# First batch of a softmax-off-by-one attention with a maxout feed-forward: denominators inverted by VectorE out of PSUM instead of by ScalarE's logarithm and exponential

## The chip, the cores and the metric

One core of one Trainium2 chip. The metric is the device time of one execution in microseconds (us); of several executions the median is given. Engines are named as in the profile: PE is TensorE, DVE is VectorE, ACT is ScalarE, POOL is GpSimd, SP is the sync engine. L12 means line 12 of the kernel before.

## What is computed

Attention over 8 batches of 12 heads, 448 positions, 64 wide, with one added to the softmax's denominator, and then a feed-forward that takes the largest of three projections. Inputs and output are f32.

```python
scores = scale * np.matmul(q, k.transpose(0, 1, 3, 2))
m = np.max(scores, axis=-1, keepdims=True)
e = np.exp(scores - m)
attn = e / (np.sum(e, axis=-1, keepdims=True) + np.exp(-m) + 1e-09)
x = np.matmul(attn, v)                      # -> (8 * 448, 768)
h = np.maximum(np.maximum(x @ w1, x @ w2), x @ w3)
out = h @ w_out
```

Multiplied through by exp(m), the denominator is the sum of exp(score) plus one, so the kernel needs no maximum. It computes exp(score) / 8 (`EDIV` = 8), so the one that is added is 1/8, and it scales the inverse by `LAMBDA` = 256, which the last step takes out again.

## The kernel before

The heads are taken in groups of four: 24 groups, three to a batch, numbered 0 to 23. Of each group the four heads lie two and two on the 128 partitions, so that four matmuls on 64 x 64 quarters of PE make one tile of scores.

The program is written out in order, without a scheduler: each engine does its instructions in the order in which the Python code issues them. Three stretches follow each other. The first (up to about 37 us) is batch 0, groups 0 to 2, written out as a list of two-letter steps (`start`, L664). The second and third do groups 3 to 23 with projection pieces in between, and a last stretch does the end of the feed-forward.

The change touches only the first stretch. There each group is done in two parts, query columns 0 to 191 and 192 to 447 (`PARTS`), so that the feed-forward of the first columns can start early. A part's steps, with the group and the part as the digits behind them:

- `S` (`scores_part`, L407): up to two score tiles into a pair of PSUM banks (`stp`), then one exponential on ACT (L419) into `eTp`. Seven tiles make four such units.
- `G` (`pair_sum`, L428): DVE adds pairs of exponentials into `eP` (L437), so that PE has fewer terms to add. One such sum in a part 0, two in a part 1.
- `D` (`den_part`, L444): PE adds up the terms by matmuls with a matrix of ones (L345), five terms of four matmuls in a part 0 and three in a part 1, into a pair of banks (`dps`, called `den`). Then ACT takes the logarithm of the sum plus 1/8 (L463) and the exponential of minus that, times 256 (L466), into `rb`, in SBUF.
- `N` (`num_part`, L471): PE multiplies exponentials with values (`num`), and DVE multiplies the result by `rb` into `xT` (L493). In a part 0 `num` lies in two single banks, in a part 1 in a pair.
- `M` (`moe`, L614): the next piece of the projections (`up_part`, L528; matmuls L537 into the single bank `p_i`, taken out by DVE at L546 or L548). A piece needs `xT` of all three groups of batch 0 for its part. The first `M1` stands after `N20`, the last numerator of part 0.
- `T` (`pe_transpose_both`, L232): transposes of keys and queries by PE, copied out by DVE (L252, L257).
- `U` and `E`: scores and sums of group 3 and later, in another form (L297, L321, L331).

The order of the steps around the change:

```python
I S000 S001 S002 S003 T1 G001 S100 S101 T2 S102 D00 G101 S103 N00 S200 S201 D10 S202 N10 G201
S203 S010 D20 S011 N20 S012 G011 S013 M1 G012 S110 S111 M1 D01 S112 G111 S113 M1 G112 N01 S210
S211 M1 D11 G211 T3 S212 S213 G212 N11 U301 M1 D21 U32 N21 M1 E312 U334 M1 T41 E334 U356 M1 E356
```

PSUM has eight banks. Two are single banks (`ps1`), shared by `trT`, `num` of part 0, `p_i` and the warm-up. Six are three pairs (`double`, L85) that are given out in turn: each score unit, denominator and part-1 numerator takes the next pair, and must wait until the reader of what lay there three turns before is done. So a denominator's pair comes free when the instruction that reads `den` ends.

Before all that, 92 matmuls on constants (L161) run while the first loads are under way. Loads are issued from POOL's queue and, for the first keys, from SP's and ACT's.

From group 3 on the denominators are inverted by `den_group` and `recip_group` (L365, L372), also a logarithm and an exponential on ACT. The change leaves those as they are.

Of the kernel before, what the change touches and what calls it, by code (L numbers as in the profile page):

```python
# [12 lines left out]
AF = mybir.ActivationFunctionType  # L13
# [3 lines left out]
MMDT = FP16  # L17
LAMBDA = 256.0
EDIV = 8.0
# [3 lines left out]
def kernel(  # L23
# [11 lines left out]
    nc = tc.nc  # L35

    B, H, S, D = q.shape
    NTOK, DM = out.shape
    DFF = moe_w1.shape[1]
    KC = 64  # L40
# [5 lines left out]
    scale = 1.0 / math.sqrt(D)  # L46
# [5 lines left out]
            name=nc.get_next_instruction_name(),  # L52
# [6 lines left out]
    cpool = ctx.enter_context(tc.tile_pool(name="const", bufs=1))  # L59
# [21 lines left out]
    def single(name, shape=(512,), dtype=FP32):  # L81
        return ps1.tile([128, *shape], dtype, tag="bank1", name=name)


    def double(name, shape=(512,), dtype=FP32):  # L85
        turn[0] += 1
        n = turn[0] % len(pair_pools)
        return pair_pools[n].tile([128, 2, *shape], dtype, tag=f"pair{n}", name=name)
# [62 lines left out]
    load_group(2, "v")  # L151
    ones16 = cpool.tile([128, KC], MMDT, name="ones16")
    nc.vector.memset(ones16, 1.0)
    WQ, WN = 23, 208
    warm16 = cpool.tile([128, S], MMDT, name="warm16")
    nc.vector.memset(warm16, 1.0)
    warm = [single("warm") for _ in range(2)]
    for _ in range(WQ):
        for r in range(2):
            for c in range(2):  # L160
                nc.tensor.matmul(  # L161
                    out=warm[r][c * KC : c * KC + KC, 0:WN],
                    lhsT=ones16[r * KC : r * KC + KC],
                    rhs=warm16[r * KC : r * KC + KC, 0:WN],
                    start=True,
                    stop=True,
                )
# [50 lines left out]
    def half(n):  # L218
        return slice(n * KC, n * KC + KC)
# [123 lines left out]
    def av_tiles(outs, weights, moving, start, stop):  # L343
        for r, c in TILES:
            nc.tensor.matmul(  # L345
                out=outs[r][half(c)],
                lhsT=weights(r, c),
                rhs=moving(r, c),
                start=start,
                stop=stop,  # L350
            )
# [92 lines left out]
    def den_part(i, part):  # L444
        st = state[i]
        q0, q1 = PARTS[part]
        nq = (q1 - q0) * KC
        eT = st["eT", part]
        dps = double("den")
        terms = [eT[:, j] for j in range(NJ)]  # L450
        if "eP" in st:
            eP, n = st.pop("eP")
            terms = [eP[:, 0], eP[:, 1]] + terms[n:]
        for n, e in enumerate(terms):
            av_tiles(
                [dps[:, r, 0:nq] for r in range(2)],
                lambda r, c: ones16[half(r)],
                lambda r, c: e[half(r), c],
                n == 0,
                n == len(terms) - 1,  # L460
            )
        rb = small.tile([128, 2, S], FP32, tag="rb", name="rb")
        nc.scalar.activation(  # L463
            out=rb[:, :, 0:nq], in_=dps[:, :, 0:nq], func=AF.Ln, bias=1.0 / EDIV
        )
        nc.scalar.activation(  # L466
            out=rb[:, :, 0:nq], in_=rb[:, :, 0:nq], func=AF.Exp, bias=math.log(LAMBDA), scale=-1.0
        )
        st["rb", part] = rb

    def num_part(i, part):  # L471
# [176 lines left out]
    def sums(i, *units):  # L648
# [6 lines left out]
        "T": pe_transpose_both,  # L655
        "S": scores_part,
        "D": den_part,
        "N": num_part,
        "M": moe,
# [298 lines left out]
    for i in range(MID, NI + 1):  # L958
        for op, j, w in ORDER if i > MID else ORDER[4:]:
            if op == "U" and i < NI:  # L960
                for_pair()
                mm = visit([(i, j)])
                n, name = ((2, "v"), (3, "k"), (3, "q"), (0, ""))[j // 2]
# [19 lines left out]
            if op == "N":  # L983
                for_pair()
                pair = num_group(i - 1)
                n = turn[0] % 2
# [206 lines left out]
    def last_piece(c0, c1, cuts, end=None):  # L1193
        def done(bank):
            nc.vector.tensor_scalar(
                out=o_last[:, c0:c1],
                in0=bank[:, 0 : c1 - c0],
                scalar1=1.0 / LAMBDA,
                scalar2=None,
                op0=ALU.mult,  # L1200
            )
            if end is not None:
                store(LATE, NT - 1, o_last[:, end], end, (nc.sync, nc.scalar))

        return plain(B // 2 - 1, NT - 1, c0, c1, cuts, done)
# [24 lines left out]
    for n in range(4):  # L1230
# [3 lines left out]
    e = (  # L1234
        last_piece(0, NW, (3,), slice(0, NW))
        + last_piece(NW, NW + NW // 2, ())
        + last_piece(NW + NW // 2, DM, (), slice(NW, DM))
    )
# [37 lines left out]
```

## Time and profile before

| what | us |
|---|---|
| median of 3 runs | 319.5 |
| lowest and highest of them | 318.58, 319.5 |
| the profiled execution, its own time | 318.78 |
| its span, from the first to the last instruction | 317.0 |
| first and last L463 start | 14.0, 34.3 |
| first and last L466 start | 14.5, 34.9 |
| last L493 start | 35.9 |
| granted TensorE clock | 1.000 |

Rows of the profile read: line, engine, operation, output <- inputs, number of instructions, busy time, mean duration of one in ns, the idle time of that engine just before, and what ended it. In rows in order of time the first two figures are the start and the length of a merged stretch. Six executions of L463 (502 to 629 ns) and six of L466 (522 to 630 ns) are what is replaced.

### The profile page before, as it was taken

The page shows a single profiled execution, that of the slowest core. Times are in us where ns is not written, and L with a number is a line of the kernel's source. Part 1 is how long each engine was busy: PE and PEld are TensorE (multiplying, and loading weights), DVE is VectorE, ACT ScalarE, POOL GpSimd, SP SyncE. Part 2 cuts the span into 40 slices and gives each one's busy share as a digit, 9 for nine tenths or more (in the row PEclk, how much of TensorE's full clock was granted, in tenths as well). Part 3 has the DMA queues.
Part 4 walks back from the last instruction along what each step waited for, and adds up shares of the span by engine and source line. Part 5 has one row for each costly group of instructions (what it writes and reads, how often), then busy time and mean ns, then how long its engine had stood idle before and what let it go on. Part 6 is the DMA issues. An engine that isn't in the chain of part 4 may idle for free.

```text
span 317.0 us, 12721 instructions
## 1 busy us (share of the span) xinstructions
PE 303.0 (96%) x5605; PEld 232.5 (73%) x5605; DVE 235.1 (74%) x434; ACT 229.6 (72%) x308; POOL 100.5 (32%) x173
## 2 busy tenths in 40 slices
PE   7679999999999999999999999999999999999993
PEld 6567777658779877788878897898887775555562
DVE  3546598999888768877776778788866746987953
ACT  1899859987778786788778986878889664654350
POOL 8967666640232332233222332333000000000040
PEclk9999999999999999999999999999999999999999
DMA  7999999999489998889995999689800052000176
GB/s 144 168 189 197 204 207 187 157 179 162 60 119 114 176 173 119 121 120 225 121 128 68 189 177 197 74 131 189 171 4 2 2 134 70 1 0 2 50 201 199
DMA packets 59927, 40.64 MB, mean 128 GB/s; under 512 B 32832, under 2 KB 56864, under 8 KB 59872
## 3 DMA queue, kind: packets, MB, share of 16 engines
q0 software_dynamic: 25680, 21.80, 48.9%
q1 hardware_dynamic: 33648, 17.21, 26.7%
q8 instruction: 44, 0.72, 1.0%
q10 hardware_dynamic: 544, 0.82, 0.8%
q14 instruction: 11, 0.09, 0.1%
HBM read 42.47 MB, written 11.01 MB: 169 GB/s over the span
## 4 chain that ended last, share of the span: by engine, by line
PE 84%; ACT 7%; issue 2%; DMA 2%; DVE 2%; POOL 1%; DVEq 0%; POOLq 0%
PE piece L785 42%; PE stp L297 9%; PE bank_a L1028 8%; PE av L345 8%; PE bank_s L1028 6%; PE p_i L537 4%; ACT eTp L419 3%; PE piece L537 2%; ACT eT L321 2%; PE bank_a L1173 2%; DMA ld_q<-in_q_dram 2%; PE den L345 1%; PE piece L560 1%; ACT rb L463 1%; DVE eS L331 1%
## 5 line engine op out<-in xcount | busy, mean ns | idle before, releaser
L321 ACT ACTIVATE eT<-stp 128x896 f16<-128x896 f32 x147 | 132.3, 918 | 33.6 <-PE stp L297 31.7
L785 PE MATMUL piece<-xT,w 64*64 64x448 f16 x2160 | 134.9, 349 | 0.4 <-DVE xT L400 0.3
L785 PEld LDWEIGHTS <-w 64*64 64x64 f16 x2160 | 93.3, 107 | 17.7 <-issue 2.8
L331 DVE TENSOR_TENSOR eS<-eS,eT 128x896 f16<-128x896 f16 x105 | 65.2, 621 | 12.5 <-ACT eT L321 10.7
L297 PE MATMUL stp<-qkT 64*64 64x448 f16 (+2 forms) x756 | 69.3, 332 | 2.3 <-ACT eTp L419 0.8
L785 PE MATMUL piece<-w,hT 64*64 64x384 f16 x792 | 48.7, 323 | 0.4 <-DVE hT L526 0.4
L526 DVE TENSOR_TENSOR hT<-hT,piece 128x448 f16<-128x448 f16 x60 | 37.1, 619 | 14.9 <-PE piece L785 12.0
L112 POOL DMA_DIRECT2D ld_q<-in_q_dram x48 | 28.9, 609 | 53.8 <-PE stp L297 24.1
L112 POOL DMA_DIRECT2D ld_v<-in_v_dram x48 | 28.5, 597 | 43.1 <-PE stp L297 25.1
L297 PEld LDWEIGHTS <-qkT 64*64 64x64 f16 x756 | 30.8, 106 | 11.3 <-issue 5.7
L785 PEld LDWEIGHTS <-hT 64*64 64x64 f16 x792 | 34.9, 107 | 4.5 <-issue 1.1
L112 POOL DMA_DIRECT2D ld_k<-in_k_dram x46 | 27.7, 608 | 23.6 <-PE stp L297 10.3
L345 PE MATMUL av<-eT,ld_v 64*64 64x448 f16 x588 | 33.0, 349 | 0.5 <-issue 0.5
L345 PEld LDWEIGHTS <-ld_v 64*64 64x64 f16 x756 | 27.3, 107 | 6.1 <-issue 1.4
L586 POOL DMA_DIRECT2D out_dram<-o x7 | 3.7, 536 | 84.0 <-DMA out_dram<-o_sb 79.3
L400 DVE TENSOR_TENSOR xT<-av,rb 128x448 f16<-128x448 f32 x42 | 24.2, 618 | 7.0 <-PE piece L785 3.5
L365 ACT ACTIVATE rb<-den 128x896 f32<-128x896 f32 x21 | 19.3, 918 | 5.6 <-PE den L345 5.5
L419 ACT ACTIVATE eTp<-stp 128x768 f16<-128x768 f32 (+3 forms) x24 | 18.0, 821 | 7.4 <-PE stp L297 7.3
L537 PEld LDWEIGHTS <-w 128*128 128x128 f16 x216 | 18.9, 98 | 5.2 <-issue 3.5
L372 ACT ACTIVATE rb<-rb 128x896 f32<-128x896 f32 x21 | 20.1, 955 | 0.2
L1028 PEld LDWEIGHTS <-comb 128*128 128x128 f16 x108 | 10.6, 98 | 9.9
L331 DVE TENSOR_TENSOR eS<-eT 128x896 f16<-128x896 f16 x21 | 13.0, 621 | 5.9 <-ACT eT L321 5.8
(102 smaller groups left out, 333.9 us busy)
## 6 DMA issues: line engine op xcount, KB each, us to landing
out_dram<-o_sb SPq DMA_DIRECT2D x42, 192.0 KB, 4.1
ld_q<-in_q_dram POOLq DMA_DIRECT2D x48, 112.0 KB, 4.3
ld_v<-in_v_dram POOLq DMA_DIRECT2D x48, 112.0 KB, 4.1
ld_k<-in_k_dram POOLq DMA_DIRECT2D x46, 112.0 KB, 4.2
w<-in_moe_w_dram POOLq DMA_DIRECT2D x6, 192.0 KB, 7.0
w<-in_moe_w_out_dram POOLq DMA_DIRECT2D x3, 384.0 KB, 7.5
w<-in_moe_w_dram POOLq DMA_DIRECT2D x2, 384.0 KB, 6.7
out_dram<-o SPq DMA_DIRECT2D x8, 96.0 KB, 3.0
```

What stands on the lines that cost most here:

```text
L112: return eng.dma_start(out=dst[hp * KC : hp * KC + KC].rearrange("p s j d -> p s (j d)"), in_=src[:, half_heads(name, hp)],)
L297: mm = nc.tensor.matmul(out=out[half(c), r], lhsT=qkT[half(r), 0, j, h], rhs=qkT[half(r), 1, q0:q1, h], start=True, stop=True,)
L321: nc.scalar.activation(out=st["eT"][:, j], in_=stp[:, :, 0:S], func=AF.Exp, scale=scale, bias=-math.log(EDIV))
L331: nc.vector.tensor_tensor(out=st["eS"], in0=st["eT"][:, 0] if j == 1 else st["eS"], in1=st["eT"][:, j], op=ALU.add,)
L345: nc.tensor.matmul(out=outs[r][half(c)], lhsT=weights(r, c), rhs=moving(r, c), start=start, stop=stop,)
L372: nc.scalar.activation(out=st["rb"], in_=st["rb"], func=AF.Exp, bias=math.log(LAMBDA), scale=-1.0)
L400: nc.vector.tensor_tensor(out=xT[b][:, 2 * g + r, :], in0=banks[r][:, 0:S], in1=state[i]["rb"][:, r], op=ALU.mult)
L419: nc.scalar.activation(out=eT[:, j0 : j0 + n].rearrange("p j r q -> p r j q"), in_=stp[:, :, 0 : n * nq].rearrange("p r (j q) -> p r j q", ...
L526: nc.vector.tensor_tensor(out=dst, in0=dst, in1=p_i[:, 0:S], op=ALU.max)
L537: nc.tensor.matmul(out=p_i[:, ts(j, nq)], lhsT=w_sb[i][:, dc, ts(2 * fp + j, 128)], rhs=xT[b][:, dc, q0 * KC : q1 * KC], start=(dc == 0), ...
L785: nc.tensor.matmul(out=p["bank"][half(c), 0:w], lhsT=lhs(k, r, c), rhs=rhs(k, r), start=(r == p["first"] and k == 0), stop=(r != p["first" ...
L1028: nc.tensor.matmul(out=bank, lhsT=lhs(k), rhs=rhs(k), start=start and k == 0, stop=k == 2, skip_group_check=True,)
```

## The change

The six pairs of ACT instructions in `den_part` go, and one DVE reciprocal, which reads the denominators in PSUM and writes `rb` in SBUF as f32, stands in their place. The 1/8 that the logarithm's bias added is now added by PE: a further term, ahead of the others, multiplies two constant tiles, and since 1/256 is folded into the matrix that was ones, the reciprocal gives the scaled inverse directly. Two new constant tiles are set by DVE at the start; the wider one also serves the warm-up matmuls, in place of the tile of 448 ones.

```diff
     ones16 = cpool.tile([128, KC], MMDT, name="ones16")
     nc.vector.memset(ones16, 1.0)
+    inv16 = cpool.tile([128, KC], MMDT, name="inv16")
+    nc.vector.memset(inv16, 1.0 / LAMBDA)
     WQ, WN = 23, 208
-    warm16 = cpool.tile([128, S], MMDT, name="warm16")
-    nc.vector.memset(warm16, 1.0)
+
+    one16 = cpool.tile([128, 4 * KC], MMDT, name="one16")
+    nc.vector.memset(one16, 1.0 / EDIV / KC)
...
-                    rhs=warm16[r * KC : r * KC + KC, 0:WN],
+                    rhs=one16[r * KC : r * KC + KC, 0:WN],
...
-        for n, e in enumerate(terms):
+        for n, e in enumerate([None, *terms]):
             av_tiles(
                 [dps[:, r, 0:nq] for r in range(2)],
-                lambda r, c: ones16[half(r)],
-                lambda r, c: e[half(r), c],
+                lambda r, c: inv16[half(r)],
+                lambda r, c: one16[half(r), 0:nq] if e is None else e[half(r), c],
                 n == 0,
-                n == len(terms) - 1,
+                n == len(terms),
             )
         rb = small.tile([128, 2, S], FP32, tag="rb", name="rb")
-        nc.scalar.activation(
-            out=rb[:, :, 0:nq], in_=dps[:, :, 0:nq], func=AF.Ln, bias=1.0 / EDIV
-        )
-        nc.scalar.activation(
-            out=rb[:, :, 0:nq], in_=rb[:, :, 0:nq], func=AF.Exp, bias=math.log(LAMBDA), scale=-1.0
-        )
+        nc.vector.reciprocal(out=rb[:, :, 0:nq], in_=dps[:, :, 0:nq])
```

No step changes its place in the list. In DVE's order the first reciprocal now stands ahead of G101's sum, the second ahead of group 1's `xT`, and each of the others between the pair sums, `hT` and `xT` instructions where `den_part` issues it.

## Prediction

> **What bounds the kernel now.** I read the page's head first, then the windows of the first 72 us, then the chain of waits of 10 to 40 us, then VectorE's and ScalarE's rows in order of time, since the change touches only the first batch. The head:
>
> ```profile
> span 317.0 us, 12721 instructions
> PE 303.0 (96%) x5605; PEld 232.5 (73%) x5605; DVE 235.1 (74%) x434; ACT 229.6 (72%) x308; POOL 100.5 (32%) x173
> ```
>
> Over the whole span TensorE (PE) is the bound. By stages (columns: stretch, its length, busy time of PE, weight loads, VectorE, ScalarE, GpSimd, granted clock, DMA share, GB/s):
>
> ```profile
> 13.70:21.20 7.50, 5.04 (x185) 3.92 (x179) 2.67 (x9) 7.41 (x14) 5.30 (x9) 1.00 1.21 175
> 21.20:36.70 15.50, 14.96 (x297) 11.59 (x296) 10.47 (x21) 14.67 (x21) 11.52 (x19) 1.00 1.25 198
> 36.70:72.00 35.30, 34.18 (x610) 23.95 (x609) 31.46 (x58) 28.93 (x35) 20.56 (x34) 1.00 1.15 186
> 72.00:260.00 188.00, 187.04 (x3990) 156.36 (x3986) 144.05 (x265) 148.05 (x188) 47.42 (x80) 1.00 0.79 123
> ```
>
> The reader is to see that the change falls in the first two rows. ScalarE is full there (22.1 of 23.0 us), VectorE has 13.1 of 23.0 busy, so 9.9 us free. From 36.7 us on PE is busy all but about 2 us of 223: what delays PE's work before 36.7 us comes out at the end nearly whole, and what is gained there is kept. The chain of waits within 10 to 40 us agrees:
>
> ```profile
> by line: ACT eTp L419 37.0%; PE p_i L537 18.6%; DMA ld_q<-in_q_dram 17.2%; issue 11.7%; ACT rb L463 7.6%; PE stp L297 7.5%; ACT rb L466 5.8%; PE den L345 3.1%; PE num L345 2.5%; DVE qkT L257 2.1%; PE trT L223 2.0%; PE trT L228 1.9%
> ```
>
> L463 and L466 are the logarithm and exponential that the change removes: 13.4% of that stretch's chain.
>
> **Removed from ScalarE.** Six pairs. One pair takes 0.97 us (384 columns, 14.01 to 14.98) or 1.2 us (512 columns, 24.72 to 25.91); read off the starts of what follows, the six sum to 6.5 us.
>
> **Added on PE.** One more term of four matmuls per part, ahead of the others. In the timeline 28 matmuls of 192 columns take 0.77 us and 28 of 256 take 0.93 to 0.96 us, so four cost 0.11 and 0.14 us: 3 x (0.11 + 0.14) = 0.75 us in all. They read constants alone and need only a free bank pair, so in the first three parts they lie in PE's waits (2.46 us idle before 21.2); the other three, 0.4 us, lie on PE. The new constants' two memsets (64 and 256 columns) stand for one of 448 columns (0.43 us at 0.98 us); the first data come at 5.25 us, so they cost nothing.
>
> **Added on VectorE: six reciprocals out of PSUM, three of 384 and three of 512 columns.** No row of this trace divides on VectorE, so the cost is bounded. One pass over the same columns is the conversion out of PSUM:
>
> ```profile
> L546 DVE CAST hT<-p_i 128x512 f16<-128x512 f32 x3 | 2.1, 692 | 1.5 <-PE p_i L537 1.4
> ...
> L546 DVE CAST hT<-p_i 128x384 f16<-128x384 f32 x3 | 1.7, 558 | 1.4 <-PE p_i L537 1.4
> ```
>
> The difference gives (692 - 558) / 128 = 1.05 ns per column and pass; the next instruction starts 0.47 us after the short one (22.35 to 22.82 us), so 0.07 us is fixed. Lower end: one pass, 0.47 and 0.61 us, six for 3.2 us. Upper end: a quotient to full f32 put together from multiplies and subtracts. From a start value good to about 4 bits, three Newton steps (4, 8, 16, more than 24 bits) of three operations are nine passes. In between: L1128 applies two operations in one pass at the same 0.56 us, so a step can be two passes, which with one for the start value makes seven. I take seven: every row of VectorE here is an add, subtract, multiply, maximum, copy or conversion, and a division is none of these but can be made of them; the nearest rows that make the same number, L463 and L466, don't do it in one instruction either. This is an estimate: 7 x 384 x 1.05 ns + 0.07 = 2.88 us, and 7 x 512 x 1.05 ns + 0.07 = 3.82 us, six for 20.1 us. Each pass more or less is 2688 columns x 1.05 ns = 2.8 us.
>
> The trace has no row for it, but the Trainium skill, "VectorE: DVE Perf Modes", section "First, the fixed hardware budget", speaks against the change: a reciprocal there is an iterative divide with a repeat count of 8. If that means eight cycles per column at the page's 0.96 GHz, the two sizes would take 3.2 and 4.3 us, 22.4 us in all, and the sum below would come to 333.0 us by it instead.
>
> **Why it lies on the path.** Each reciprocal stands in VectorE's queue ahead of work that PE waits for. Before, this was the gap in which VectorE waited for ScalarE:
>
> ```profile
> 13.66 0.55 DVE L437 TENSOR_TENSOR eP<-eTp 128x768 f16<-128x768 f16 x1
> 15.10 0.62 DVE L493 TENSOR_TENSOR xT<-num,rb 128x192 f16<-128x192 f32 x2 [0.90 <-ACT rb L466]
> 17.82 0.62 DVE L493 TENSOR_TENSOR xT<-num,rb 128x192 f16<-128x192 f32 x2 [2.09 <-ACT rb L466]
> 18.36 0.55 DVE L437 TENSOR_TENSOR eP<-eTp 128x768 f16<-128x768 f16 x1
> 20.75 0.62 DVE L493 TENSOR_TENSOR xT<-num,rb 128x192 f16<-128x192 f32 x2 [1.84 <-ACT rb L466]
> ```
>
> In the changed order a part's reciprocal comes before the next part's pair sum (eP), which that next part's denominator needs; so the parts become one chain, reciprocal, pair sum, denominator, reciprocal. Also the pair of banks stays taken until the reciprocal ends. Worked through with the times of before for all other instructions (matmul groups 0.5 us for a denominator, 1.1 us for a projection piece, 0.65 us for two score tiles; VectorE 0.5 to 0.6 us each):
>
> - Group 0, part 0: denominators done at 13.7, reciprocal 13.8 to 16.7; pair sum of group 1 to 17.2, two xT to 17.8; denominator to 17.8.
> - Group 1: reciprocal 17.9 to 20.8, xT 21.4, pair sum of group 2 21.9, denominator 22.5.
> - Group 2: reciprocal 22.5 to 25.4, xT 26.0, where before it ended at 21.4: 4.6 us late. Now two pieces and two score tiles, denominator at 29.4.
> - Group 0, part 1: reciprocal 29.4 to 33.2; queued behind it pair sum, hT, pair sum, then xT to 35.6 (before 28.3: 7.3 us late). The numerator waits for the same bank pair until 33.2, then scores and a piece; denominator of group 1 at 36.5.
> - Group 1: reciprocal 36.5 to 40.3; behind it a pair sum, the two copies of group 3's transposes (1.1 us), a pair sum, xT to 43.3 (before 33.1: 10.2 us late). Scores, a piece, denominator at 44.1.
> - Group 2: reciprocal 44.2 to 48.0, xT 48.7. The score tile after it takes the reciprocal's banks at 48.05, and the piece after that ends at 50.1, where before it ended at 38.18: 11.9 us late.
>
> A check by throughput: VectorE's 13.1 us of old work and 20.1 us of new make 33.2 us where 23.0 were there, 10.2 us late without any wait. The chain's 11.9 adds the waits for PE. After this point the orders are the same, and PE has 1.1 us of idle time up to 72 us and about 1 us up to 260, so I give nothing back. The sum is made against the profiled execution, 318.78 us with a span of 317.0: 318.78 + 11.9 = **330.7 us**. The median of the runs shown is 319.5, 0.7 above; I don't add it. ScalarE's 6.5 us buys nothing, since VectorE is late in its place.
>
> **Rivals.**
>
> *One pass (the other side).* If a reciprocal runs at the rate of L546, 3.2 us fit into VectorE's 9.9 us of idle time, and the chain loses ScalarE's pairs. The score exponential at 14.98 starts at 14.0, the second denominator ends at 15.4, the third at 18.3, xT of group 2 at 19.9 and not 21.4: 1.5 us. After that PE is nearly full; its score groups that wait for ScalarE (0.83 for 0.50 us at 24.38, 0.87 for 0.57 at 31.79, and 0.26 idle) give 0.9, less 0.4 for the new terms: 0.5. That gives 316.8 us. For it: one-pass rows are all that VectorE shows, and ScalarE bounds that stretch. Against it: none of them divides. It decides below 2.8 passes, where 11.9 - (7 - n) x 2.8 reaches zero, that is below about 1.2 and 1.6 us for the two sizes.
>
> *Three to five passes.* Slower still, but the free 9.9 us take most of it: at four passes 11.9 - 8.4 = 3.5, so 322.3 us.
>
> *The order costs nothing over the throughput.* If later work fills the chain's gaps, or PE gives 1 to 2 us back after 36.7, 318.78 + 10.2 = 329.0 us. It lies in the forecast's range.
>
> *The change does not do what it says* in one point that could be: ScalarE's freed time might go unused, as PE is full from 21.2 on. With one-pass reciprocals that leaves 1.1 us of the gain, 317.7; with long ones nothing changes.
>
> **How the numbers follow.** Five to nine passes: 318.78 + 6.3 = 325 to 318.78 + 17.5 = 336; chance 0.80 with the gap-filling rival in it. One pass up to the turning point: 0.13. Between that and five: 0.06. Above nine: 0.01. The range is 325 to 336, which leaves 2 in 10 out. About 0.3%, 1 us, is what a measurement of this kernel can tell from no change; that is a third of a pass to either side of 2.8, chance 0.02, taken out of these cases. Faster 0.12, within 0.02, slower 0.86.
>
> **What would show it.** Right: rows of a reciprocal rb<-den of 2.5 to 3.6 us (384 columns) and 3.3 to 4.8 us (512); VectorE at 9 tenths in the page's second to sixth slices, PE and ScalarE lower there; waits of PE and of VectorE's followers for the reciprocal at the top of the list; the last xT of the first batch (L493 before) near 48.7 us and the rest shifted by 12 us. Wrong: reciprocal rows near 0.55 us, or a stage after 36.7 us that is shorter than the 35.3 us of before by more than 2 us, so that the delay is given back.

## The result, and the profile after

The changed kernel takes 330.48 us (median of 6 runs, 328.1 to 334.49), the kernel before 319.5 us (6 runs beside them, 318.58 to 319.99): a ratio of 1.0336, 95% interval 1.0291 to 1.0381. A second series of the same kernel gave 330.97 against 319.23, 1.0354 (1.0318 to 1.0390). Executions of a kernel can fall into a slower state, and the ratios here compare the means of the other executions alone: they leave out the 334.49 us and, below, one execution each of "part 0 alone" and "sums ahead". 330.7 was forecast.

That the number fits does not yet say that its terms do. Two executions of the changed kernel were profiled, one of 332.12 us (span 330.3) and one of 328.01 us (span 326.2). The changed file's lines are shifted: the reciprocal is L466, denominators and numerators L348, scores L300, projection pieces L535, `xT` L491, pair sums L440, the loads of the weights L186 to L188. The head of the page of the first:

```profile
span 330.3 us, 12761 instructions
PE 307.5 (93%) x5629; PEld 241.3 (73%) x5629; DVE 252.3 (76%) x441; ACT 224.6 (68%) x296; POOL 100.5 (30%) x173
```

VectorE has 17.2 us more, ScalarE 5 us less, PE 24 matmuls more (six terms of four). The same windows as before the change, of this first execution:

```profile
13.70:21.20 7.50, 5.95 (x176) 5.33 (x172) 5.22 (x7) 4.71 (x7) 6.52 (x11) 0.75 1.13 148
21.20:36.70 15.50, 10.27 (x220) 8.52 (x209) 13.28 (x15) 7.96 (x10) 9.98 (x17) 0.89 1.26 198
36.70:72.00 35.30, 30.47 (x596) 23.14 (x588) 31.38 (x49) 23.14 (x28) 14.96 (x25) 1.00 0.84 138
```

ScalarE, full before, is now half idle; VectorE is the busiest in the second row; PE stands still for 5.2 of 15.5 us there. One column was not in the forecast: PE's granted clock, 0.75 and 0.89 where it was 1.00. The chain of waits from 10 to 52 us has the reciprocal in front:

```profile
by line: DVE rb L466 42.4%; DMA ld_q<-in_q_dram 15.1%; PE p_i L535 14.0%; PE stp L300 9.5%; PE den L348 6.5%; PE trT L226 6.2%; DVE qkT L260 3.1%; issue 2.8%; DVE hT L546 2.6%; DVE eP L440 2.4%; DVE xT L491 2.4%; PE num L348 2.3%; PE trT L2
```

The reciprocal's own rows (number, then shortest, median and longest in ns):

```profile
L466 DVE RECIPROCAL rb<-den x6: 2557/2958/3359, 17.0 to 45.9; 128x384 f32<-128x384 f32 x3, 128x512 f32<-128x512 f32 x3
```

384 columns take 2.56 us and 512 take 3.36, so (3359 - 2557) / 128 = 6.3 ns per column: six passes of 1.05 ns, not seven. Now VectorE in order of time, in the second profiled execution, whose first instructions ran as in the kernel before (left column: start):

```profile
13.71 2.56 DVE L466 RECIPROCAL rb<-den 128x384 f32<-128x384 f32 x1 [0.17 <-PE den L348]
16.18 0.49 DVE L440 TENSOR_TENSOR eP<-eTp 128x768 f16<-128x768 f16 x1
16.60 0.61 DVE L491 TENSOR_TENSOR xT<-num,rb 128x192 f16<-128x192 f32 x2
17.39 2.56 DVE L466 RECIPROCAL rb<-den 128x384 f32<-128x384 f32 x1 [0.18 <-PE den L348]
20.05 0.62 DVE L491 TENSOR_TENSOR xT<-num,rb 128x192 f16<-128x192 f32 x2
20.59 0.55 DVE L440 TENSOR_TENSOR eP<-eTp 128x768 f16<-128x768 f16 x1
22.25 2.56 DVE L466 RECIPROCAL rb<-den 128x384 f32<-128x384 f32 x1 [1.11 <-PE den L348]
```

This is the forecast's chain: reciprocal, pair sum, `xT`, a wait for the next denominator, which waited for that pair sum, reciprocal. The denominator's wait is in PE's rows:

```profile
21.19 0.53 PE L348 MATMUL den<-eP,inv 64*64 64x192 f16 x8 [0.39 <-DVE eP L440]
```

PE's side of it in the same execution: the next score tile and, in part 1, the numerator wait for the reciprocal, because it holds their bank pair.

```profile
PE stp L300 <- DVE rb L466: 5.3, 4, 1.8
...
PE num L348 <- DVE rb L466: 4.0, 2, 2.1
```

| | forecast | second execution | before |
|---|---|---|---|
| starts of the six reciprocals | 13.8, 17.9, 22.5, 29.4, 36.5, 44.2 | 13.7, 17.4, 22.3, 28.8, 35.3, 42.6 | |
| end of the seventh projection piece | 50.1 | 48.0 (46.48 + 1.48) | 38.2 |
| late by | 11.9 | 9.8 | |
| span | | 326.2 | 317.0 |

Of the 9.8 us, 9.2 arrive at the end (326.2 - 317.0): PE gave 0.6 us back. Not all of the 9.8 us are waits. With the reciprocals as measured, VectorE's own time is 13.1 + 17.2 us for the 23.0 us that were there, which is 7.3 us late without any wait; 2.5 us are left for the waits between the engines, PE's clock and the added term. (From the start of the first reciprocal to that of the seventh piece VectorE is busy 29.4 of 32.8 us.)

The first execution is 4.1 us longer than the second. Its first reciprocal starts at 17.05 and not at 13.71 us, so 3.3 us of that lie ahead of every instruction that the change made long. From that start to the start of the seventh piece both executions take 32.8 us (17.05 to 49.82 and 13.71 to 46.48). PE ahead of the first reciprocal:

```profile
8.99 0.58 PE L226 MATMUL trT<-ident,ld_k 128*64 128x128 f16 x14
11.40 0.96 PE L226 MATMUL trT<-ident,ld_q 128*64 128x128 f16 x14 [1.83 <-DMA ld_q<-in_q_dram]
13.08 0.85 PE L300 MATMUL stp<-qkT 64*64 64x192 f16 x16 [0.72 <-DVE qkT L260]
```

The second group's queries came 1.5 us later (11.40 against 9.88 us), PE stood idle for 1.8 us, and the next 14 transposes took 0.96 us where the 14 before took 0.58. The granted clock was 0.50 from about 10.6 to 17 us. The reciprocals come later than this load and cannot have delayed it; "term only" below, which has the same instructions up to that point, had a mean clock of 0.990 to 0.998 in its runs, and the kernel before 0.988 to 1.000 in the runs beside. The changed kernel's mean clock is lower, 0.973 to 0.993 in its twelve runs. The second execution's clock, too, was at 0.50, from about 18 to 24 us, and the first one's again from 24.3 to 27.7, behind waits for the reciprocals.

### The profile page after: what moved, and what is told of

Its sections match the earlier page's. It is cut to its first block, busy times and chain, and to the rows that moved or that the text cites. A ratio compares the mean times of both kernels' runs of the same rounds, so it can differ in the third digit from the quotient of the medians.

```text
span 330.3 us, 12761 instructions
## 1 busy us (share of the span) xinstructions
PE 307.5 (93%) x5629; PEld 241.3 (73%) x5629; DVE 252.3 (76%) x441; ACT 224.6 (68%) x296; POOL 100.5 (30%) x173
## 4 chain that ended last, share of the span: by engine, by line
PE 83%; DVE 8%; ACT 3%; DMA 2%; issue 1%; POOL 1%; DVEq 0%; POOLq 0%
PE piece L783 41%; PE stp L300 9%; PE bank_a L1026 8%; PE av L348 8%; PE bank_s L1026 6%; DVE rb L466 5%; PE p_i L535 4%; PE piece L535 2%; DMA ld_q<-in_q_dram 2%; PE den L348 2%; ACT eT L324 2%; PE bank_a L1171 2%; PE piece L558 1%; PE trT L226 1%; DVE eS L334 1%
## 5 line engine op out<-in xcount | busy, mean ns | idle before, releaser
L783 PEld LDWEIGHTS <-w 64*64 64x64 f16 x2160 | 97.0, 107 | 15.0 <-issue 3.6
L300 PE MATMUL stp<-qkT 64*64 64x448 f16 (+2 forms) x756 | 70.9, 339 | 7.3 <-DVE rb L466 5.5
L300 PEld LDWEIGHTS <-qkT 64*64 64x64 f16 x756 | 31.8, 109 | 15.9 <-issue 9.9
L348 PEld LDWEIGHTS <-ld_v 64*64 64x64 f16 x756 | 29.1, 111 | 8.5 <-issue 4.5
L348 PE MATMUL av<-eT,ld_v 64*64 64x448 f16 x588 | 32.9, 349 | 0.0
L422 ACT ACTIVATE eTp<-stp 128x768 f16<-128x768 f32 (+3 forms) x24 | 18.8, 823 | 20.6 <-PE stp L300 15.7
L535 PEld LDWEIGHTS <-w 128*128 128x128 f16 x216 | 18.9, 98 | 5.1 <-issue 3.2
L375 ACT ACTIVATE rb<-rb 128x896 f32<-128x896 f32 x21 | 20.1, 955 | 0.2
L466 DVE RECIPROCAL rb<-den 128x384 f32<-128x384 f32 (+1 forms) x6 | 17.7, 2958 | 2.2 <-PE den L348 2.1
L1026 PEld LDWEIGHTS <-comb 128*128 128x128 f16 x108 | 10.6, 98 | 9.9
```

The source lines that it names most:

```text
L300: mm = nc.tensor.matmul(out=out[half(c), r], lhsT=qkT[half(r), 0, j, h], rhs=qkT[half(r), 1, q0:q1, h], start=True, stop=True,)
L348: nc.tensor.matmul(out=outs[r][half(c)], lhsT=weights(r, c), rhs=moving(r, c), start=start, stop=stop,)
L375: nc.scalar.activation(out=st["rb"], in_=st["rb"], func=AF.Exp, bias=math.log(LAMBDA), scale=-1.0)
L466: nc.vector.reciprocal(out=rb[:, :, 0:nq], in_=dps[:, :, 0:nq])
L535: nc.tensor.matmul(out=p_i[:, ts(j, nq)], lhsT=w_sb[i][:, dc, ts(2 * fp + j, 128)], rhs=xT[b][:, dc, q0 * KC : q1 * KC], start=(dc == 0), ...
L783: nc.tensor.matmul(out=p["bank"][half(c), 0:w], lhsT=lhs(k, r, c), rhs=rhs(k, r), start=(r == p["first"] and k == 0), stop=(r != p["first" ...
```

## The experiments

My theory after the result: the reciprocals' length on VectorE, six times, chained by VectorE's order and the bank pairs. Rivals: the added term; the place and not the length; VectorE's time alone, whatever the order; PE's clock.

**Term only.** ScalarE keeps its two functions, on the denominators that PE now completes.

```diff
-        nc.vector.reciprocal(out=rb[:, :, 0:nq], in_=dps[:, :, 0:nq])
+        nc.scalar.activation(out=rb[:, :, 0:nq], in_=dps[:, :, 0:nq], func=AF.Ln)
+        nc.scalar.activation(out=rb[:, :, 0:nq], in_=rb[:, :, 0:nq], func=AF.Exp, scale=-1.0)
```

> The added term by a matmul and the folded 1/256 as in the change, but ScalarE still makes the inverse by a logarithm and an exponential. Theory (the long reciprocals are the whole loss): the three terms of part 0 lie in waits of PE, the other three cost 0.4 us, so 319.9 us, within 0.3% of before, clock near 1.00. Rival (the term, or the constants' memsets, hurt by themselves): 322 us or more.

320.05 us against 319.06, ratio 1.0046 (1.0022 to 1.0071). So the term with its constants costs about 1 us by the medians, more than the 0.4 us of the forecast (why is not shown), but a tenth of the change. The rival falls.

**One pass.** A copy in the reciprocal's place.

```diff
-        nc.vector.reciprocal(out=rb[:, :, 0:nq], in_=dps[:, :, 0:nq])
+        nc.vector.tensor_copy(out=rb[:, :, 0:nq], in_=dps[:, :, 0:nq])
```

> As the change, but a VectorE copy out of PSUM takes the place of each reciprocal, so the division is left out (the numerators are multiplied by the denominators). Rows of 0.56 and 0.69 us. Theory (the reciprocal's length decides, not its place): the 3.2 us fit into VectorE's idle time and ScalarE's six pairs go, 317 to 318 us. Rival (the place in VectorE's queue or the bank pair held by VectorE is what hurts): 321 us or more.

319.23 us against 319.06, ratio 0.9999 (0.9972 to 1.0027). With a short instruction (0.56 and 0.69 us) in the same place, holding the same bank pair, nothing is lost: the length decides, and the rival falls. That the place costs nothing at all is not shown, since ScalarE's freed time and the added term are in the same sum. The expected gain of 1 to 2 us did not come either, and the profile of this one execution shows a wait that takes it. PE in order of time:

```profile
18.87 0.36 PE L348 MATMUL den<-eP,inv 64*64 64x192 f16 x8 [0.75 <-DVE eP L440]
...
20.71 1.15 PE L535 MATMUL p_i<-xT,w 128*128 128x192 f16 x12
...
22.36 0.26 PE L535 MATMUL p_i<-xT,w 128*128 128x192 f16 x1
23.97 1.08 PE L535 MATMUL p_i<-xT,w 128*128 128x192 f16 x11 [1.35 <-DMA w<-in_moe_w_dram]
```

The third denominator still waits for its pair sum. The first piece starts 0.45 us earlier than before (21.16), and the second stops after one matmul for 1.35 us, for its weights. So the weights' transfer is the next limit in line. In the trace of the kernel before it already had no slack: the last transfer of the second piece's weights was issued at 15.3 us and took 7.7 us, and that piece began at 22.94. Here it landed about a microsecond later, and so it did in "term only", where ScalarE's pairs are kept; that microsecond is not the work of the copy. The seventh piece starts at 37.40 us, before at 36.70.

**One part each.** Reciprocals in part 0 alone, and in part 1 alone; the other part as in "term only".

```diff
-        nc.vector.reciprocal(out=rb[:, :, 0:nq], in_=dps[:, :, 0:nq])
+        if part == 0:    # in the other kernel: part == 1
+            nc.vector.reciprocal(out=rb[:, :, 0:nq], in_=dps[:, :, 0:nq])
+        else:
+            ...
```

> Reciprocals by VectorE in part 0 only (three of 384 columns, 2.5 us each), ScalarE's pair in part 1. Theory (chain through pair sums and banks): xT of the third group about 3.4 us late, so 322 to 324 us. Rival (throughput alone): 7.5 us of new work into 9.9 us of idle time, 319.5 to 320 us.

> Reciprocals by VectorE in part 1 only (three of 512 columns, 3.3 us each). In the trace of the change the stretch from the first to the seventh projection piece is 21.2 us long, before it was 15.5, so the chain gives 5.6 us more than before: 325 us. With the part-0 half the two losses should add up to that of the whole change (8 to 11 us) if one does not hide in the other. Rival (the clock, which fell in the first 28 us of the change, makes most of the loss): 321 to 322 us.

Part 0 alone: 324.51 us, 1.0162 (1.0126 to 1.0199), 5.4 us over 319.06. Part 1 alone: 326.78 us, 1.0227 (1.0195 to 1.0259), 7.7 us. The first refutes that free time anywhere in the stretch takes up the new work: 7.5 us of it, 9.9 us free, and yet 5.4 us lost. It does not refute VectorE's own time as the larger part: within part 0 itself (13.7 to 21.2 us) VectorE had only 7.50 - 2.67 = 4.8 us free, so 2.7 us are lost there without any wait, and the first piece starts 3.8 us late (25.00 for 21.16). Both times are above what I expected, and their sum, about 13 us, is above the whole change's 11 to 11.7. In both profiles PE's clock is at 0.50 for some 7 us (21.8 to 28.6 and 36.2 to 43), and the first piece in the part-0 kernel takes 2.08 us for the usual 1.15; that fits one such loss in each half, but a count of them in the other runs was not made.

**Twice.** Each reciprocal issued a second time over the first (`for _ in range(2)` around it).

> Each of the six reciprocals issued twice, the second over the first. Theory (all of a reciprocal lies on the chain): the six new ones, 17.2 us in all, come out whole, 347 to 349 us, and up to 4 us more where PE's clock falls in the longer waits. Rival (some of VectorE's time still hides in waits): 342 us or less.

354.12 us, 1.1094 (1.1061 to 1.1127): 23.2 us over the change's 330.97, measured beside it. The new reciprocals are 17.8 us (VectorE's busy time, 269.6 for 251.8), 17.2 by the expectation; the loss is larger than that, so the rival falls. The other 5.4 us are more than expected. VectorE and then PE in this execution (its lines are one further on):

```profile
27.86 5.15 DVE L467 RECIPROCAL rb<-den 128x384 f32<-128x384 f32 x2 [1.12 <-PE den L348]
...
35.64 0.56 DVE L545 CAST hT<-p_i 128x384 f16<-128x384 f32 x1 [1.31 <-PE p_i L536]
```

```profile
33.52 2.08 PE L536 MATMUL p_i<-xT,w 128*128 128x192 f16 x12
36.51 1.16 PE L536 MATMUL p_i<-xT,w 128*128 128x192 f16 x12
...
69.51 2.74 PE L536 MATMUL p_i<-xT,w 128*128 128x256 f16 x12
```

After a pause of PE behind a reciprocal pair, the same twelve matmuls take 2.08 us and not 1.16, 2.74 and not 1.48, and VectorE, in turn, waits longer for them. The mean granted clock is 0.955.

**Bank pair free early.** ScalarE copies the denominators out, VectorE inverts in SBUF.

```diff
-        nc.vector.reciprocal(out=rb[:, :, 0:nq], in_=dps[:, :, 0:nq])
+        nc.scalar.activation(out=rb[:, :, 0:nq], in_=dps[:, :, 0:nq], func=AF.Copy)
+        nc.vector.reciprocal(out=rb[:, :, 0:nq], in_=rb[:, :, 0:nq])
```

> ScalarE copies the denominators from PSUM to SBUF (0.5 and 0.6 us), VectorE inverts them there: the bank pair comes free early, the reciprocals keep their length and their place in VectorE's queue. Rival (the held bank pairs are the mechanism; the list of waits of the change gives PE 9.5 us of waits for the reciprocal): those waits go, 321 to 324 us. Theory (VectorE's queue is the mechanism, the pair sum behind each reciprocal becomes the next wait): 328 to 331 us.

334.06 us, 1.0471 (1.0440 to 1.0502): slower than the change. The waits for the bank are gone, as meant, and others stand in their place (engine and line, what it waited for, us in total, times, longest):

```profile
DVE rb L467 <- ACT rb L466: 5.6, 6, 1.6
PE den L348 <- DVE eP L440: 5.1, 2, 2.8
...
PE stp L300 <- DVE qkT L260: 3.6, 1, 3.6
```

PE now waits for the pair sum and for the transposes' copy, which stand behind the reciprocals, and ScalarE's copy of the denominators lies ahead of each reciprocal. In SBUF the reciprocal is no shorter (2552 and 3353 ns). The rival that the held banks are the mechanism by themselves falls: even without the 5.6 us in which VectorE waits for ScalarE's copy it would be 328.5 us, by an estimate that takes them as wholly lost, and not 321 to 324. The size was missed, 334 for 328 to 331.

**PE kept busy.** Each part-0 numerator computed twice (`for j in [*range(NJ)] * (2 if part == 0 else 1)`).

> As the change, but each part-0 numerator is computed twice into the same banks, so that PE has 0.8 us more to do where it waits for a reciprocal. If part of the loss is PE's clock, which was at 0.5 from 24.2 to 27.7 us in the change, the clock stays up there and the time is 0.5 to 1 us below that of the change; if the clock costs nothing on the chain, the time is the same or up to 1 us above.

330.27 us, 1.0355 (1.0321 to 1.0389), beside the change's 330.97 with 1.0354: no difference. In the profile the clock did stay at 1.00 from 15 us on, where the second execution of the change has 0.50 from 18 to 24 us, and from the first reciprocal to the first piece it takes 11.25 us (15.0 to 26.25) in place of 11.61 (13.71 to 25.32). At the start of the seventh piece the difference is the same (15.04 to 47.40 is 32.4 us, for 32.8). So behind the first reciprocal the fall of the clock costs about 0.4 us, one execution against another; but in this execution the clock fell earlier, between 11 and 15 us, and the time gives no verdict.

**The change again**, beside these.

> The change itself once more, beside the three kernels of this call: 328 to 332 us. A second profile tells whether the late first loads (the second group's queries landed at 11.3 us, before at 10.1) belong to the change or to that one execution; if to the execution, the clock drop at 10.5 to 17.5 us goes with them and the time is near 328 us.

330.97 us, and the profile shown above: the late queries belong to the execution, not to the change: this one had none, and took the 328 us that were expected. It is also the fastest of its six.

**Pair sums ahead, and both.** The order of four steps changed, with the reciprocals out of PSUM, and with those in SBUF.

```diff
-S102 D00 G101 S103 N00 S200 S201 D10 S202 N10 G201
+S102 G101 D00 S103 N00 S200 S201 G201 D10 S202 N10
...
-D01 S112 G111 S113 M1 G112 N01 S210 S211 M1 D11 G211 T3
+G111 D01 S112 S113 M1 G112 N01 S210 S211 M1 G211 D11 T3
```

> The change with four pair sums issued ahead of the reciprocal that they stood behind (the first sum of the next group, in both parts), nothing else moved. If the pair sum behind the reciprocal is the link of the chain, part 0 shortens by about 1 us a group and the time falls 2 to 3 us below the change, to 328 us. If the held bank pair is the link as well (the next score tile and the numerators wait for it), part 1 gains nothing, and the whole is 329 to 331 us.

> The denominators copied to SBUF by ScalarE and inverted there (bank pairs free early), with the four pair sums ahead of the reciprocals as well. Neither link alone is enough; with both eased, VectorE's own time is the bound: 13.1 us old, 17.2 us reciprocals against 23.0 us, and about 1 us for the copy ahead of the first one, so 7 to 9 us over before, 326 to 328 us. If it is still above 330 us, waits remain that this account does not name.

Sums ahead: 332.30 us, 1.0384 (1.0344 to 1.0424). Both: 330.57 us, 1.0341 (1.0306 to 1.0376). Neither differs from the change (1.0336 and 1.0354) clear of noise. "Both" lies above the 326 to 328 us of VectorE's time alone, and above the 330 us from which, by its own expectation, waits remain that this account does not name. With both links eased the reciprocals of part 0 do stand nearly back to back:

```profile
17.71 2.55 DVE L467 RECIPROCAL rb<-rb 128x384 f32<-128x384 f32 x1 [0.87 <-ACT rb L466]
...
21.37 2.54 DVE L467 RECIPROCAL rb<-rb 128x384 f32<-128x384 f32 x1
...
24.56 2.54 DVE L467 RECIPROCAL rb<-rb 128x384 f32<-128x384 f32 x1
```

From the first to the third that is 6.9 us, 7.9 with the sums ahead alone, 8.5 in the change. The gain is lost behind them. With both, PE stands still for 3 us behind the fifth reciprocal, until VectorE has copied out the transposes of group 3, which were not moved ahead of it, and the piece after that runs at the low clock:

```profile
42.59 0.96 PE L300 MATMUL stp<-qkT 64*64 64x448 f16 x8 [2.98 <-DVE qkT L260]
43.49 2.10 PE L536 MATMUL p_i<-xT,w 128*128 128x192 f16 x12
```

In the kernel with the sums ahead, PE after the third reciprocal:

```profile
25.81 2.08 PE L535 MATMUL p_i<-xT,w 128*128 128x192 f16 x12
27.82 1.07 PE L300 MATMUL stp<-qkT 64*64 64x256 f16 x16
28.82 1.61 PE L535 MATMUL p_i<-xT,w 128*128 128x192 f16 x12
```

The same three stretches took 1.15, 0.63 and 1.16 us in the change's second execution: the clock was at 0.50 from 23 to about 29.5 us. No version tried beats the kernel before, and with "one pass" at no gain (0.9972 to 1.0027) not even a reciprocal of one pass would, in this order.

## Why the prediction was right

- **The stage and what it is worth.** Right. A delay of the seventh piece of 9.8 us came out as 9.2 at the end, so giving nothing back was 0.6 us too strict. Doubling the reciprocals cost more than their length, and with a one-pass copy in their place there is no loss: it is their length that costs.
- **The chain.** Right in its links, which the rows above show one by one, but it does not carry the whole loss. Of the 9.8 us at the seventh piece, VectorE's own time makes 7.3 by the sum above; the forecast's own check by throughput had it so, 10.2 of 11.9. What each link is worth is not shown. The SBUF kernel eases the banks, the sums-ahead kernel the order, the last one both, and none gains: other waits behind the reciprocals take their place, in the last one for the transposes' copies (2.98 us), which the account had not named as a link.
- **"I take seven".** Too large. Six passes (6.3 ns per column) make the six reciprocals 17.2 us of VectorE's queue (2.47 and 3.27 us from start to next start) and not 20.1. No run shows how the reciprocal is made, so the working by Newton steps stays unshown, and that it came within one pass is in part luck. By the forecast's own 2.8 us per pass it is 318.78 + 11.9 - 2.8 = 327.9 us, and the execution whose first loads came in time took 328.01. The Trainium skill, "VectorE: DVE Perf Modes", section "First, the fixed hardware budget", read as eight cycles per column, would have been further off: at that page's 0.96 GHz (section "Specifications") the measured 6.3 ns are six cycles.
- **What was left out: PE's clock.** The forecast took every matmul at the durations of before. Behind the reciprocals the clock falls to 0.50 for some microseconds; in the second execution that is worth about 0.4 us, by the kernel with doubled numerators, whose clock stayed up there. The medians, 11.0 and 11.7 us over before, are about 2 us more than the 9.2 between two single executions. What makes these 2 us is not shown. That it is the clock is argued: runs with a lower mean clock tend to be longer (in "PE kept busy" 328.75 us at 0.992 and 331.67 at 0.982), but 328.1 and 330.2 us of the first series both stand at 0.987, and where the first execution was longer, most of it lay at a late load ahead of the first reciprocal. So the forecast's 330.7 meets 330.48 by luck: one pass too many, 2.8 us too long, and about 2 us that the forecast did not have.
- **The added term.** 0.4 us forecast, 1.0 us measured by the medians (the ratio's interval, 1.0022 to 1.0071 of 319.06, is 0.7 to 2.3 us). The run holds the term together with the constants' memsets, which were put at nothing.
- **The one-pass rival.** A short instruction in that place loses nothing, as it said; its price, 316.8 us, was wrong (319.23). It moved the bound from ScalarE to PE and forgot the second piece's weights, which in the kernel before landed just as that piece began. At one pass, below its turning point of 2.8, there is no gain.
- **Its signs.** The reciprocal's rows, 2.56 and 3.36 us, lie just inside the lower ends that were named. The last `xT` of the first batch ends at 46.8 us and not 48.7, and the rest is shifted by 9 to 10 us and not 12. VectorE is not at 9 tenths in the second to sixth slices but at 6, 8, 8, 9 and 8 (second execution), and the longest wait in the list is ScalarE's for scores (6.8 us), ahead of PE's two for the reciprocal (5.3 and 4.0).

## What to carry to other kernels

An instruction put on an engine with free time can still cost most of its length where it stands ahead of a short instruction that another engine waits for, or holds the buffer that the next step needs: here 17.2 us of reciprocals cost 9 to 12 with 9.9 us free. Count the free time of the stage in which the result is needed, and draw the chain through the queue and the buffers as well. Price an operation that no row shows from both sides, and then ask what is next in line on the winning side too: here, in the execution profiled, it was a transfer. And where a step makes TensorE pause, its next matmuls may not run at the speed of the rows of before.

## What the runs showed of the hardware that was not expected

VectorE's reciprocal of f32 takes 6.3 ns per column, out of PSUM (2557 and 3359 ns for 384 and 512 columns) as out of SBUF (2552 and 3353), against 1.05 ns for a conversion. TensorE's granted clock fell to 0.50 around pauses much shorter than the stretch it then lasted: in the first profiled execution PE was busy 1.75 of the 4 us from 8 to 12 us, and the clock was at 0.50 from 10.6 to 17 us, though PE was busy from 14 on; twelve 128x192 matmuls took 2.08 us at it, and 1.15 at full clock. In the kernel before, with no pause over 1.3 us in that stretch of the profiled execution, it stayed at 1.00. A longer pause does not always bring it down: in both executions of the change PE waited 1.85 and 2.11 us for the fourth and fifth reciprocals, and the clock stayed at 1.00. These runs give no rule for when it falls.
